# Float32 from the two words of a double: an integer add on Pool in place of two VectorE instructions

## The chip, the cores and the metric

The kernel runs on one core of a Trainium2 chip. Such a core has TensorE (matmuls), VectorE, ScalarE and Pool (GpSimd), which work side by side, each through its own instructions in order, and wait for each other by semaphores; SyncE issues the transfers. In the profile they are PE, DVE, ACT, POOL and SP. The metric is the time of one execution on the device in microseconds. The kernel before takes 1402.88 us, the median of three runs (1402.10 to 1403.73).

## The reference

Attention in chunks of 64 positions, then two feed-forward layers. The weights come as float64; the output is float32.

```python
scores = scale * np.matmul(q_c, k_c.transpose(0, 1, 2, 4, 3))   # 8 x 8 heads, 9 chunks of 64, head_dim 64
scores = scores - np.max(scores, axis=-1, keepdims=True)
attn = np.exp(scores)
attn = attn / (np.sum(attn, axis=-1, keepdims=True) + 1e-09)
out = np.matmul(attn, v_c)
x = out.transpose(0, 2, 1, 3).reshape(4608, 512)
h = np.maximum(np.maximum(x @ w1, x @ w2), x @ w3)               # 512 x 768 each
y = h @ w_out                                                    # 768 x 512
h = np.maximum(y @ w_in, 0.0)                                    # 512 x 2048
out = h * h @ w_out2                                             # 2048 x 512
```

## The kernel before, in words

The 4608 tokens are nine blocks of 512. A float32 operand is kept as two parts, hi (rounded to TensorE's fp32r) and lo (the rest), and a product of two operands is three matmuls: hi·hi, hi·lo, lo·hi. All weights are cut into tiles of 128 x 512: 24 for phase 1 (for each of six slices f of d_ff, three of w1, w2, w3 and one of w_out), 32 for phase 2 (w_in and w_out2).

**A weight tile** comes from HBM as `raw`, 128 x 512 pairs of 32-bit words: w0 is the low word of the double, w1 the high word. `convert` (L91 to L123) makes float32 of them. It is a generator; each `yield` ends a step, and the code that drives it decides what stands between two steps. In order: ScalarE takes the absolute value of the high word (Abs, L103); VectorE clamps it (L105), shifts it by 3 bits (L107) and puts the sign and the top exponent bit back (L110), which gives `a`, the value cut off below the high word's bits; ScalarE copies `a` to hi (L112); VectorE takes a's sign and exponent (L114) and multiplies the low word, as a number, by them (L116), which gives `s`; Pool subtracts hi from `a` (L122) and adds `s` (L123), which gives lo. For a tile of phase 2 (`hi is None`) Pool adds `s` to `a` in two halves (L120).

**The first phase** (everything up to about 185 us) is in the order in which it is written; a scheduler orders what comes later. For each of the first eight attention tiles there is a loop (L619 to L648): xl of the tile before (L341, VectorE), the transpose T of the softmax numerators e (L307, TensorE), a maximum (L285) and its subtraction (L288) two tiles ahead, three steps of a weight tile, a chunk of the products p, the products X (L330), scores S three tiles ahead, the sum of the next tile's e (L295) and its reciprocal rs (L298, L300), Pool's e*rs (L301), which the next T needs, the last steps of the weight tile, and Abs of the next one. ScalarE copies T to SBUF (et, L311) and X to xh (L336).

**Behind the loops** `flow` takes the other 16 tiles of phase 1 through their steps, three or four steps for each chunk of 24 matmuls: in a tile's third step, after L110 and hi, it also issues Abs of the next tile. Between the steps stand the ends of the products: for w1 ScalarE's copy s (L383), for w2 the maximum m (L386), for w3 the maximum h (L390), its hi part hh (L392, ScalarE) and hl (L394). Products p have two PSUM banks, so a chunk waits until the end of the one before the last has been read. y (L355 too) are the products with w_out.

Then come phase 2's operands (parked in HBM and fetched back), and its products z (L449) and o (L500). Temporary tiles of `convert`, s, m and h rotate through eight buffers.

Of the kernel before, what the change touches and what calls it, by code (L numbers as in the profile page):

```python
# [9 lines left out]
F32 = mybir.dt.float32  # L10
F32R = mybir.dt.float32r
BF16 = mybir.dt.bfloat16
U32 = mybir.dt.uint32
AF = mybir.ActivationFunctionType
ALU = mybir.AluOpType
# [26 lines left out]
def kernel(ctx: ExitStack, tc, qkv, w123, w_out, w_in2, w_out2, out):  # L42


    nc = tc.nc
# [10 lines left out]
    def tmp(name):  # L56
        return ap.tile([P, 512], F32, tag="t", name=name, bufs=NTMP)
# [24 lines left out]
    def halved(t):  # L82
        return t.rearrange("p (a c) -> p a c", a=2)
# [6 lines left out]

    def convert(raw, hi, lo):  # L91

        w0, w1 = raw[:, :, 0], raw[:, :, 1]
        a = tmp("a")
        s = tmp("s")  # L100
        au, su = a.bitcast(U32), s.bitcast(U32)
        v = nc.vector
        nc.scalar.activation(a, w1.bitcast(F32), AF.Abs)  # L103
        yield
        v.tensor_scalar(out=a, in0=a, scalar1=E_INF, scalar2=E_ZERO, op0=ALU.min, op1=ALU.max)  # L105
        yield
        v.tensor_scalar(out=au, in0=au, scalar1=3, scalar2=0x3FFFFFFF,  # L107
                        op0=ALU.logical_shift_left, op1=ALU.bitwise_and)
        yield
        v.scalar_tensor_tensor(out=au, in0=w1, scalar=0xC0000000, in1=au, op0=ALU.bitwise_and, op1=ALU.bitwise_or)  # L110
        if hi is not None:
            nc.scalar.copy(hi, halved(a))  # L112
        yield
        v.tensor_scalar(out=su, in0=au, scalar1=0xFF800000, scalar2=None, op0=ALU.bitwise_and)  # L114
        yield
        v.scalar_tensor_tensor(out=s, in0=w0, scalar=2.0**-52, in1=s, op0=ALU.mult, op1=ALU.mult)  # L116
        if hi is None:
            for h, part in enumerate(lo):
                c = slice(h * HC, h * HC + HC)
                nc.gpsimd.tensor_tensor(out=part, in0=a[:, c], in1=s[:, c], op=ALU.add)  # L120
            return
        nc.gpsimd.tensor_tensor(out=halved(a), in0=halved(a), in1=hi.bitcast(F32), op=ALU.subtract)  # L122
        nc.gpsimd.tensor_tensor(out=lo, in0=halved(a), in1=halved(s), op=ALU.add)  # L123

    def unit_steps(src, name, keep, late=False):


        if late:
            hi, lo = [shifted(name + n).rearrange("p (a c) -> p a c", a=2)[:, :, SH:] for n in "hl"]
        else:  # L130
            hi, lo = [halved(wp.tile([P, 512], F32R, tag="w", name=name + n)) for n in "hl"]
        keep(hi, lo)
        if src.dtype == F32:
            raw = ap.tile([P, 512], F32, tag="in", name="raw", bufs=4)
            nc.sync.dma_start(raw, src)
            yield
            split(halved(raw), hi, lo)
        else:
            raw = ap.tile([P, 512, 2], U32, tag="in", name="raw", bufs=4)
            nc.sync.dma_start(raw.rearrange("p n w -> p (n w)"), src.bitcast(U32))  # L140
            yield
            yield from convert(raw, hi, lo)
# [38 lines left out]
    def park(n, g):  # L181

        src = (lambda f: w_in2[f]) if n == "wi" else (lambda f: w_out2[f * P:(f + 1) * P, :])
        d = parked[n, g] = dp.tile([7, 2, P, 512], F32, name=f"{n}{g}d")
        q = [halved((level if n == "wi" and i < N0 else operand)(f"q{i}").bitcast(F32)) for i in range(4)]

        for r in range(2):
            for a in range(2):
                s, parts = src(2 * g + a + 8 * r), [x[:, a, :] for x in q[2 * r:2 * r + 2]]
                if s.dtype == F32:  # L190
                    for h in range(2):
                        nc.sync.dma_start(parts[h], s[:, h * HC:h * HC + HC])
                    yield
                else:
                    raw = ap.tile([P, 512, 2], U32, tag="in", name="raw", bufs=4)
                    nc.sync.dma_start(raw.rearrange("p n w -> p (n w)"), s.bitcast(U32))
                    yield
                    for k, _ in enumerate(convert(raw, None, parts)):
                        if k in (0, 2):
                            yield  # L200
                    yield
        for i, x in combine(q, n == "wi", nc.gpsimd):
            yield
            hi, lo = operand("ph"), operand("pl")
            nc.scalar.copy(halved(hi), x)
            yield
            nc.vector.tensor_tensor(out=halved(lo), in0=x, in1=halved(hi).bitcast(F32), op=ALU.subtract)  # L207
            nc.sync.dma_start(d[i - 1, 0], hi.bitcast(F32))
            nc.sync.dma_start(d[i - 1, 1], lo.bitcast(F32))
# [245 lines left out]
    def take(tag, name):  # L455
        t = tmp(name)
        nc.scalar.copy(t, bank[tag])  # L457
        return t
# [279 lines left out]
    for b in range(NB):  # L738
        for g in range(NG):
            bank["at"] = None  # L740
            z(b, g, 1, "at", True)
            a, s1 = bank["at"], take("at", "s1")
# [97 lines left out]
```

## Time and profile before

| | |
|---|---|
| median of 3 runs | 1402.88 us (1402.10 to 1403.73) |
| span of the profiled execution | 1401.4 us |
| TensorE busy | 1376.2 us (98%) |
| VectorE busy | 963.6 us (69%) |
| ScalarE busy | 492.4 us (35%) |
| Pool busy | 237.4 us (17%) |

The span runs from the first to the last instruction. Busy shares are means over stages with different limits: VectorE's 69% is 95% in one stage and far less in others. A wait is read from a row's end, "[3.26 <-ACT s L383]": the engine sat idle for 3.26 us before this instruction, until ScalarE's instruction of line 383, which wrote s, was done.

### The profile page before, as it was taken

What the parts mean: (1) busy time and instruction counts of PE and PEld (TensorE: products, weight loads), DVE (VectorE), ACT (ScalarE), POOL (GpSimd) and SP (SyncE); (2) the same over time, 40 slices, a digit from 0 to 9 for tenths busy, and PEclk for the clock granted to TensorE, in tenths of its full rate; (3) what the DMA queues carried; (4) which work ended last, traced back from release to release, by engine and by line L of the source; (5) the groups of instructions that cost most, each with busy time, mean ns of one, the idle gap of its engine ahead of it and who ended that gap; (6) DMA issues with size and microseconds to landing.
All of it is one profiled execution on the core that took longest, in us unless ns stands there. A gap on an engine that the chain in (4) does not pass through costs nothing.

```text
span 1401.4 us, 32734 instructions
## 1 busy us (share of the span) xinstructions
PE 1376.2 (98%) x13719; PEld 1358.6 (97%) x13719; DVE 963.6 (69%) x1525; ACT 492.4 (35%) x848; POOL 237.4 (17%) x204
## 2 busy tenths in 40 slices
PE   8889999999999999999999999999999999999998
PEld 5889999999999999999999999999999999999998
DVE  7998657677758577723266666666677888877774
ACT  3433233332323332411133333333334444444442
POOL 3654213332514323300000000000000000000000
PEclk9999999999999999999999999999999999999999
DMA  9332244653735554626643343343498444334341
GB/s 281 100 103 91 95 133 136 219 174 106 263 129 174 196 189 137 248 70 212 195 146 134 136 149 139 136 149 138 178 350 307 144 143 137 128 129 150 123 140 41
DMA packets 101236, 222.33 MB, mean 159 GB/s; under 512 B 11232, under 2 KB 20448, under 8 KB 101088
## 3 DMA queue, kind: packets, MB, share of 16 engines
q1 hardware_dynamic: 101088, 220.25, 46.1%
q8 instruction: 107, 1.75, 0.5%
q14 instruction: 41, 0.34, 0.1%
HBM read 134.22 MB, written 85.98 MB: 157 GB/s over the span
## 4 chain that ended last, share of the span: by engine, by line
PE 85%; DVE 1%; issue 0%; POOLq 0%; POOL 0%; ACT 0%; DVEq 0%; ACTq 0%
PE o L500 25%; PE z L449 25%; PE p L355 24%; PE y L355 9%; PE X L330 1%; PE S L278 1%; PE T L307 1%; DVE pl L207 0%; DVE u L472 0%; POOL u L472 0%; POOLq L836 0%; DVE mx L285 0%; DVE sm L295 0%; DVE e L288 0%; DVE h L390 0%
## 5 line engine op out<-in xcount | busy, mean ns | idle before, releaser
L449 PE MATMUL z<-yxh,wih 128*128 128x256 f32 x560 | 154.9, 277 | 0.0
L449 PE MATMUL z<-yxh,wil 128*128 128x256 f32 x560 | 154.7, 276 | 0.0
L449 PE MATMUL z<-yxl,wih 128*128 128x256 f32 x560 | 154.7, 276 | 0.0
L500 PE MATMUL o<-wo2h,gl 128*128 128x256 f32 x504 | 140.7, 279 | 0.0
L472 POOL TENSOR_TENSOR u<-u,s 128x512 f32<-128x512 f32 x9 | 11.7, 1296 | 761.5 <-DVE u L472 761.5
L500 PE MATMUL o<-wo2h,gh 128*128 128x256 f32 x504 | 140.4, 279 | 0.0
L500 PE MATMUL o<-wo2l,gh 128*128 128x256 f32 x504 | 140.2, 278 | 0.0
L500 PE MATMUL o<-wo2h,gxl 128*128 128x256 f32 x504 | 140.1, 278 | 0.0
L500 PE MATMUL o<-wo2h,gxh 128*128 128x256 f32 x504 | 139.9, 278 | 0.0
L500 PE MATMUL o<-wo2l,gxh 128*128 128x256 f32 x504 | 139.9, 278 | 0.0
L472 DVE TENSOR_TENSOR c<-z,s 128x512 f32<-128x512 f32 x108 | 74.3, 688 | 89.2 <-PE z L449 84.7
L449 PE MATMUL z<-yh,wih 128*128 128x256 f32 x448 | 124.2, 277 | 0.0
L449 PE MATMUL z<-yh,wil 128*128 128x256 f32 x448 | 124.1, 277 | 0.0
L449 PE MATMUL z<-yl,wih 128*128 128x256 f32 x448 | 124.1, 277 | 0.0
L392 ACT CAST hh<-h 128x512 fp32r<-128x512 f32 x54 | 33.5, 621 | 220.4 <-DVE h L390 209.4
L390 DVE TENSOR_TENSOR h<-p,m 128x512 f32<-128x512 f32 x54 | 37.1, 687 | 107.0 <-PE p L355 107.0
L457 ACT COPY s<-z 128x512 f32<-128x512 f32 x108 | 63.3, 586 | 133.7 <-PE z L449 132.4
L449 PEld LDWEIGHTS z<-yxh,wih 128*128 128x128 f32 x560 | 105.2, 188 | 0.2 <-DVE c L472 0.2
L449 PEld LDWEIGHTS z<-yxh,wil 128*128 128x128 f32 x560 | 105.1, 188 | 0.0
L449 PEld LDWEIGHTS z<-yxl,wih 128*128 128x128 f32 x560 | 105.1, 188 | 0.0
L500 PEld LDWEIGHTS o<-wo2l,gh 128*128 128x128 f32 x504 | 94.9, 188 | 0.0
L500 PEld LDWEIGHTS o<-wo2h,gl 128*128 128x128 f32 x504 | 94.7, 188 | 0.0
(196 smaller groups left out, 4160.1 us busy)
## 6 DMA issues: line engine op xcount, KB each, us to landing
gd<-g SPq DMA_DIRECT2D x144, 256.0 KB, 2.0
gr<-gd SPq DMA_DIRECT2D x72, 512.0 KB, 4.2
qk<-in_qkv SPq DMA_DIRECT2D x28, 512.0 KB, 4.3
raw<-in_w_out SPq DMA_DIRECT2D x22, 512.0 KB, 5.0
raw<-in_w SPq DMA_DIRECT2D x18, 512.0 KB, 3.5
v<-in_qkv SPq DMA_DIRECT2D x72, 128.0 KB, 5.9
yd<-ys SPq DMA_DIRECT2D x36, 256.0 KB, 2.8
yr<-yd SPq DMA_DIRECT2D x18, 512.0 KB, 5.0
```

Source lines behind the costliest of these rows:

```text
L278: nc.tensor.matmul(s_t[t][o:o + D, h ^ t % 2, :], lhsT=q[r, h, :], rhs=k[r, h, :], start=True, stop=True,)
L307: nc.tensor.transpose(tp[:, p * P:(p + 1) * P], e[:, 2 * p:2 * p + 2, :].rearrange("p h k -> p (h k)"), ident)
L330: nc.tensor.matmul(xps_t[t][j * D:j * D + D, p, c * D:c * D + D], lhsT=v[o:o + D, c, p, :], rhs=et[o:o + D, p, q:q + D], start=True, stop= ...
L355: nc.tensor.matmul(dst[:, c], lhsT=lhs, rhs=rhs[:, c], start=first and i == 0 and j == 0, stop=last and j == len(pairs) - 1, skip_group_ch ...
L390: nc.vector.tensor_tensor(out=h, in0=p, in1=st[b], op=ALU.max)
L392: nc.scalar.copy(hh, h)
L449: nc.tensor.matmul(dst[:, a * HC:a * HC + HC], lhsT=l[:, a, w], rhs=r[:, k, :], start=first and a + k + j == 0, stop=j == 2, skip_group_ch ...
L457: nc.scalar.copy(t, bank[tag])
L472: (eng or nc.vector).tensor_tensor(out=t, in0=x, in1=y, op=ALU.add)
L500: nc.tensor.matmul(bank[i][:, m * HC:m * HC + HC], lhsT=l[:, a, t], rhs=r[:, a, :], start=g + m + a + j == 0, stop=g == NG - 1 and j == 2, ...
```

## The change

`convert` no longer makes `s`. ScalarE copies the low word, as a number, times 2 to the power -29, to an integer tile `r` (this is the rounded carry into the low bits of the float32); Pool adds `r` to the bits of `a` as integers; only then does ScalarE copy hi, and Pool subtracts hi from the sum. VectorE's L114 and L116 go. A tile's conversion has one step less, so its last step is empty where the loops and `flow` still take it.

```diff
         w0, w1 = raw[:, :, 0], raw[:, :, 1]
         a = tmp("a")
-        s = tmp("s")
-        au, su = a.bitcast(U32), s.bitcast(U32)
+        r = tmp("r")
+        au, ru = a.bitcast(U32), r.bitcast(U32)
         v = nc.vector
         nc.scalar.activation(a, w1.bitcast(F32), AF.Abs)
+        nc.scalar.activation(ru, w0, AF.Copy, scale=2.0**-29)
         yield
...
         v.scalar_tensor_tensor(out=au, in0=w1, scalar=0xC0000000, in1=au, op0=ALU.bitwise_and, op1=ALU.bitwise_or)
-        if hi is not None:
-            nc.scalar.copy(hi, halved(a))
-        yield
-        v.tensor_scalar(out=su, in0=au, scalar1=0xFF800000, scalar2=None, op0=ALU.bitwise_and)
-        yield
-        v.scalar_tensor_tensor(out=s, in0=w0, scalar=2.0**-52, in1=s, op0=ALU.mult, op1=ALU.mult)
         if hi is None:
             for h, part in enumerate(lo):
                 c = slice(h * HC, h * HC + HC)
-                nc.gpsimd.tensor_tensor(out=part, in0=a[:, c], in1=s[:, c], op=ALU.add)
+                nc.gpsimd.tensor_tensor(out=part.bitcast(U32), in0=au[:, c], in1=ru[:, c], op=ALU.add)
             return
-        nc.gpsimd.tensor_tensor(out=halved(a), in0=halved(a), in1=hi.bitcast(F32), op=ALU.subtract)
-        nc.gpsimd.tensor_tensor(out=lo, in0=halved(a), in1=halved(s), op=ALU.add)
+        nc.gpsimd.tensor_tensor(out=au, in0=au, in1=ru, op=ALU.add)
+        nc.scalar.copy(hi, halved(a))
+        yield
+        nc.gpsimd.tensor_tensor(out=lo, in0=halved(a), in1=hi.bitcast(F32), op=ALU.subtract)
```

What this moves on Pool, in the attention loops. Before (e and rs belong to the softmax; w0_0, w1_0, w2_0 are the first three weight tiles):

```order
L301 TENSOR_TENSOR e_198<-e_198,rs_211 128x512
L301 TENSOR_TENSOR e_208<-e_208,rs_301 128x512
L122 TENSOR_TENSOR a_201<-a_201,w0_0h_119 128x512
L123 TENSOR_TENSOR w0_0l_120<-a_201,s_202 128x512
L301 TENSOR_TENSOR e_258<-e_258,rs_384 128x512
L122 TENSOR_TENSOR a_308<-a_308,w1_0h_133 128x512
L123 TENSOR_TENSOR w1_0l_134<-a_308,s_309 128x2x256
```

The same place in the changed kernel, where line 112 is the integer add, 115 the subtraction and 293 the product e*rs:

```order
L293 TENSOR_TENSOR e_198<-e_198,rs_212 128x512
L112 TENSOR_TENSOR a_201<-a_201,r_202 128x512
L115 TENSOR_TENSOR w0_0l_120<-a_201,w0_0h_119 128x512
L293 TENSOR_TENSOR e_209<-e_209,rs_303 128x512
L112 TENSOR_TENSOR a_307<-a_307,r_308 128x512
L115 TENSOR_TENSOR w1_0l_134<-a_307,w1_0h_133 128x2x256
L293 TENSOR_TENSOR e_260<-e_260,rs_385 128x512
```

A loop's e*rs stood ahead of the tile's two instructions and now stands behind them.

On ScalarE, behind the loops, before (L112 is hi, L103 the next tile's Abs, L383 the copy s, L392 hh):

```order
L112 CAST w0_2h_752<-a_935 128x512
L103 ACTIVATE a_1003<-raw_859 128x512
L383 COPY s1_1040<-p0_861 128x512
L112 CAST w1_2h_857<-a_1003 128x2x256
L103 ACTIVATE a_1045<-raw_940 128x512
L112 CAST w2_2h_938<-a_1045 128x512
L103 ACTIVATE a_1112<-raw_1037 128x512
L392 CAST hh_1118<-h_1116 128x512
```

And in the changed kernel (L113 is hi, L98 Abs, L99 the new copy, L375 s, L384 hh):

```order
L113 CAST w0_2h_747<-a_927 128x512
L98 ACTIVATE a_997<-raw_853 128x512
L99 ACTIVATE r_998<-raw_853 128x512
L375 COPY s1_1032<-p0_855 128x512
L113 CAST w1_2h_851<-a_997 128x2x256
L98 ACTIVATE a_1038<-raw_933 128x512
L99 ACTIVATE r_1039<-raw_933 128x512
L113 CAST w2_2h_931<-a_1038 128x512
L98 ACTIVATE a_1104<-raw_1029 128x512
L99 ACTIVATE r_1105<-raw_1029 128x512
L384 CAST hh_1111<-h_1109 128x512
```

Their sequence is kept and one copy comes in for each tile; hi, at the head of it, now follows Pool's add and no longer VectorE's L110.

## Rows read from the trace of the kernel before

**Rows 1.** The page, busy us, share of the span and instructions of each engine

```profile
PE 1376.2 (98%) x13719; PEld 1358.6 (97%) x13719; DVE 963.6 (69%) x1525; ACT 492.4 (35%) x848; POOL 237.4 (17%) x204
```

**Rows 2.** Windows: length, busy time of each engine, granted clock, DMA share, GB/s

```profile
60.00:120.00 60.00, 51.18 (x428) 49.91 (x427) 56.93 (x73) 20.34 (x36) 32.47 (x22) 0.94 0.32 102
120.00:155.00 35.00, 34.35 (x352) 33.95 (x351) 26.99 (x39) 9.63 (x16) 16.63 (x12) 1.00 0.27 84
155.00:700.00 545.00, 543.95 (x6190) 538.09 (x6189) 326.19 (x542) 160.95 (x284) 134.76 (x124) 1.00 0.51 169
```

**Rows 3.** Waits, 0 to 155 us: who waited for whom, total, times, longest

```profile
PE T L307 <- POOL e L301: 6.8, 5, 2.6
```

**Rows 4.** Timeline of TensorE: start, us, instruction, idle time before it

```profile
30.49 0.77 PE L307 MATMUL T<-ident,e 128*128 128x128 f32 x4 [2.55 <-POOL e L301]
...
57.19 0.66 PE L307 MATMUL T<-ident,e 128*128 128x128 f32 x4 [0.52 <-POOL e L301]
...
84.54 0.51 PE L355 MATMUL p<-xh,w_1h 128*128 128x256 f32 x2 [3.26 <-ACT s L383]
...
116.34 0.79 PE L355 MATMUL p<-xh,w_3h 128*128 128x256 f32 x2 [2.29 <-ACT s L383]
```

**Rows 5.** Timeline of VectorE, one attention loop

```profile
26.97 0.69 DVE L110 SCALAR_TENSOR_TENSOR a<-raw,a 128x512 uint32<-128x512 uint32 x1
...
28.78 0.20 DVE L300 RECIPROCAL rs<-sm 128x8 f32<-128x8 f32 x1
...
30.65 1.30 DVE L105 TENSOR_SCALAR a<-a 128x512 f32<-128x512 f32 x1
...
33.42 0.69 DVE L110 SCALAR_TENSOR_TENSOR a<-raw,a 128x512 uint32<-128x512 uint32 x1
```

**Rows 6.** Timeline of Pool, the same loop

```profile
29.06 1.38 POOL L301 TENSOR_TENSOR e<-e,rs 128x512 f32<-128x512 f32 x1 [2.41 <-DVE rs L300]
30.40 1.27 POOL L122 TENSOR_TENSOR a<-a,w_0h 128x512 f32<-128x512 f32 x1
31.75 1.34 POOL L123 TENSOR_TENSOR w_0l<-a,s 128x512 fp32r<-128x512 f32 x1
```

**Rows 7.** Timeline of all engines, one tile behind the loops

```profile
65.71 0.41 DVE L105 TENSOR_SCALAR a<-a 128x512 f32<-128x512 f32 x1
...
66.61 0.69 DVE L110 SCALAR_TENSOR_TENSOR a<-raw,a 128x512 uint32<-128x512 uint32 x1
...
67.34 0.62 ACT L112 CAST w_2h<-a 128x512 fp32r<-128x512 f32 x1 [3.95 <-DVE a L110]
67.41 0.43 DVE L114 TENSOR_SCALAR s<-a 128x512 uint32<-128x512 uint32 x1
...
67.87 0.71 ACT L103 ACTIVATE a<-raw 128x512 f32<-128x512 f32 x1
...
68.04 1.68 POOL L122 TENSOR_TENSOR a<-a,w_2h 128x512 f32<-128x512 f32 x1 [3.40 <-ACT w_2h L112]
...
68.61 1.40 DVE L105 TENSOR_SCALAR a<-a 128x512 f32<-128x512 f32 x1
...
71.47 0.69 DVE L110 SCALAR_TENSOR_TENSOR a<-raw,a 128x512 uint32<-128x512 uint32 x1
```

**Rows 8.** Groups by line, 0 to 560 us: busy us, mean ns

```profile
L116 DVE SCALAR_TENSOR_TENSOR s<-raw,s 128x512 f32<-128x512 uint32 x56 | 45.9, 830 | 0.5
...
L103 ACT ACTIVATE a<-raw 128x512 f32<-128x512 f32 x56 | 37.3, 673 | 43.2 <-DMA raw<-in_w_in 21.3 <-DMA raw<-in_w_out 13.2 <-issue 7.8
...
L114 DVE TENSOR_SCALAR s<-a 128x512 uint32<-128x512 uint32 x56 | 25.0, 466 | 1.0
```

**Rows 9.** Timeline of VectorE and ScalarE: a copy s, a later L110

```profile
82.10 0.69 DVE L110 SCALAR_TENSOR_TENSOR a<-raw,a 128x512 uint32<-128x512 uint32 x1
...
83.92 0.57 ACT L383 COPY s<-p 128x512 f32<-128x512 f32 x1
...
118.65 0.69 DVE L110 SCALAR_TENSOR_TENSOR a<-raw,a 128x512 uint32<-128x512 uint32 x1
```

## The prediction, made before the changed kernel had run

> **What bounds the kernel now.** I read the busy table first: TensorE is busy for 1376.2 of 1401.4 us [rows 1], so everything there is to win or lose lies in some 25 us of its idle time and in any new idle time. The windows say where [rows 2]: from 155 us on TensorE is busy for 543.95 of 545 us; from 60 to 120 us it is busy for only 51.18 of 60, and VectorE there for 56.93, with a granted clock of 0.94. The first 155 us are the stretch that decides. Two of its waits matter: the transposes T wait for Pool's product e*rs, 6.8 us in five waits [rows 3], and the products p wait for ScalarE's copy s. Single waits are in [rows 4]: T at 30.49 waited 2.55 us; p at 84.54 and at 116.34 waited 3.26 and 2.29 us for s, and behind the second one a pair of matmuls takes 0.79 us, against 0.51 behind the first, which is the lower clock level (1.2 GHz). So in this stretch TensorE follows VectorE, which converts the 24 weight tiles of phase 1, one after another, between the attention steps and the maxima.
>
> **What the change does to a tile.** VectorE loses the mask L114 and the product L116: 25.0 + 45.9 us over 56 tiles [rows 8], start to start some 0.9 us a tile in the attention loops, and 1.1 us (67.41 is L114's start, 68.61 the next tile's L105) later on. ScalarE gains one copy of a tile with a stride, as L103, which takes 673 ns [rows 8], about 0.53 us start to start. Pool keeps two instructions a tile, but the add comes first, then ScalarE's copy hi, then the subtraction. Three consequences, all of order and not of load:
> 1. hi now waits for Pool's add, and on ScalarE the next tile's Abs stands right behind hi. Before, hi needed only L110.
> 2. In the loops Pool's e*rs stands behind the add and the subtraction of the tile, where it stood ahead of both.
> 3. xh and s, on ScalarE behind hi, wait as well.
>
> The new add is in no row. The nearest are Pool's float32 instructions of two full inputs: 1.27 to 1.35 us alone, 1.68 when a VectorE instruction interferes [rows 6, 7]. Far ends: 0.69, VectorE's own two-input L110, and 2.7, twice the 1.34 of a Pool row, if integers are added in two passes. I take 1.3, the row it is nearest to. The Trainium skill (GPSIMD Engine Reference, Performance versus the Vector engine) puts a two-input Pool loop at about 2.6 cycles an element because both reads share a port, and that floor does not depend on the arithmetic; an estimate from it is 512 x 2.6 / 1.2 GHz = 1.11 us, and with it the sum below would come out some 4 us lower. No run here shows an integer add.
>
> **The attention loops (11 to 65 us).** Count from the start of L110 in one loop. Before: e*rs starts at 29.06 - 26.97 = 2.1 us, T at 30.49 - 26.97 = 3.5 us, and the next L110 comes at 33.42, 6.45 later [rows 4, 5, 6]. After: the add starts when L110 (0.69) is done and 0.2 has passed, at 0.9, and ends at 2.2; hi takes 2.25 to 2.87; the subtraction 2.95 to 4.25; e*rs 4.3 to 5.65; T starts at 5.7. T is thus 2.2 us later against L110. On VectorE the loop goes: xh on ScalarE behind hi, 2.78 to 3.37; xl at 3.42; the maximum at 4.02; L105 at 4.62. There e*rs is running, and L105 is held by a running Pool instruction: it takes 1.30 at 30.65 and 1.40 at 68.61, in each case to 0.3 past Pool's end, but 0.41 with Pool idle [rows 5, 6, 7]. So L105 ends at 5.95; the subtraction of the maximum at 5.87, L107 at 6.47, next L110 at 6.93. The loop grows from 6.45 to 6.93, although VectorE has 0.9 us less to do: it now waits for xh. Seven loops give 7 x 0.48 = 3.4 us (my walk, loop by loop, gives 3.2, as the first loops lose less and the fifth more, where the maximum m waits for products behind the late T). The eighth T then stands at 57.19 + 3.2 + 2.2, some 5.5 us later, and TensorE's idle time ahead of the T grows to 1.4 to 2.6 us each, so the clock may drop more than once. The first product that needs all of X, and the L110 of the next tile (66.61 before [rows 7]), come at about +5.1: VectorE has caught up a little.
>
> **The sixteen tiles behind the loops (66 to 150 us).** Before, one tile takes 71.47 - 66.61 = 4.86 us where nothing else stands between, all of it VectorE's [rows 7]; hi starts at +0.73, the next Abs at +1.26 and ends at +1.97, while VectorE is still in L116: Abs is never late. After, from L110's start: add 0.9 to 2.2, hi at 2.25, Abs at 2.78 to 3.45, L105 at 3.5. Pool's subtraction, begun at 2.95 when hi is done, is then running, stretched to 1.68 as at 68.04, so L105 ends at 4.9; L107 takes 0.46 start to start, and L110 comes at 5.4. The ring L110, add, hi, Abs, L105, L107, L110 passes through three engines and takes 5.4 us a tile in place of 4.86. Maxima and subtractions of phase 1 that stand behind L110 use VectorE's idle time and cost nothing; those between L105 and L110, and an hl that waits for an hh behind the late hi, lengthen a tile to 6.0 to 6.9. For the ten tiles from 66.61 to 118.65 [rows 7, 9] I get five at 5.4 and five at 6.0 to 6.9, 59.1 us against 52.05: +7. Last, a copy s behind hi, Abs and the new copy leaves at 3.8 after L110; at 83.92 it left 1.8 after the L110 at 82.10 [rows 9]: +2.0 for the product that waits for its buffer, as the one at 116.34 does. So at that point TensorE is 5.1 + 7 + 2 = 14 us late, with waits of 5 us or so at the places of the 3.26 and 2.29.
>
> **Behind it.** From 120 us TensorE is busy 34.35 of 35 and then all the time [rows 2]; nothing there gives the delay back. The 32 tiles of phase 2's weights gain and lose the same instructions under products that keep TensorE busy; its whole idle time from 155 to 700 us is 1.05 us, so at most that can be won, and without that cover a tile would cost the ring's 0.5 us. I cost them at nothing.
>
> **The sum.** 1401.4 + 14 = 1415.4 us for the span. The profiled span stands 1.5 us under the median of the runs, 1402.88, which has what lies around it; so I forecast 1417 us. With the add at 1.27 and hand-overs at 0.08 (28.78 + 0.20 to Pool's 29.06) in place of 0.2, 22 tiles give 3 us back; with the add at 1.68 they take 8 more: its own range is 1411 to 1426.
>
> **Rivals.**
> - *VectorE's relief pays.* For it: VectorE is 95% busy from 60 to 120 us, and TensorE's waits trail it. If nothing replaces it, some 18 tiles up to 120 us give back 0.9 each, 16 us, at most: 1387; half of it, 1395, is likelier, as TensorE then bounds. Against it: the next Abs stands behind hi, which waits for Pool, in the order of ScalarE's instructions. Chance 0.10.
> - *The port is not in the way.* If L105 starts between Pool's two instructions, at 0.41, the tile's ring is 4.4, under the 4.86 of before; ten tiles win 4.6 us and the loop is 6.0, so that the later T and the s cost about what is won: 1401 to 1406. Against it: every L105 in [rows 5, 7] that met Pool at work was held. Chance 0.08.
> - *The integer add is slow*, at 2.7 us. Then each of the 22 tiles takes 1.4 longer, 31 us: about 1448. For it: no integer instruction of Pool stands in the trace. Chance 0.08.
> - The forecast has 0.74. That the change does not do what it says can't be: in its order of instructions no L114 or L116 is left, and the new copy stands there for all 56 tiles.
>
> **How the numbers follow.** The first rival is faster by more than 0.2%, 2.8 us, about what can be told from no change; the second is split, mostly within it; the other two are slower. That makes 0.10, 0.07 and 0.83. The range, 1404 to 1428, holds the forecast with its unknown add and part of the second rival, and leaves out the first and the third.
>
> **What would show it.** Right: VectorE's busy time falls by some 70 us in all and its share from 60 to 120 us to about three quarters, with L105 waiting for ScalarE's Abs; hi waits for Pool; T waits for e*rs by 2 us and more in each loop; TensorE's idle time is near 38 us, all of the gain of it ahead of 155 us; L110 to L110 is 5.4 us or more. Wrong: VectorE's tiles follow each other in under 4.8 us, or L105 takes 0.4 beside Pool (second rival), or the add's row is far from 1.3.

## The result, and the profile after

The changed kernel takes 1413.07 us, the median of four runs (1411.27 to 1414.47), against 1402.83 us for the kernel before beside it (1402.10 to 1403.73): a ratio of 1.0064, with a 95% interval of 1.0049 to 1.0078. It is slower by 10 us. The forecast was 1417 us, the range 1404 to 1428.

The page of the kernel after (busy us, share of the span, instructions), to be held against [rows 1]; its span is 1410.0 us:

```profile
PE 1375.9 (98%) x13719; PEld 1358.2 (96%) x13719; DVE 892.6 (63%) x1413; ACT 521.0 (37%) x904; POOL 223.3 (16%) x204
```

VectorE has lost 71.0 us of work and TensorE has the same 13719 matmuls in about the same busy time, but the span is 8.6 us longer: TensorE's idle time went from 25.2 to 34.1 us. The windows of the kernel after (length, busy time of each engine, granted clock, DMA share, GB/s), beside [rows 2], say where:

```profile
60.00:120.00 60.00, 50.17 (x432) 48.76 (x432) 29.92 (x47) 23.29 (x41) 27.32 (x21) 0.94 0.30 91
120.00:155.00 35.00, 30.60 (x236) 30.40 (x237) 15.20 (x26) 13.59 (x24) 14.33 (x12) 0.90 0.28 89
155.00:700.00 545.00, 543.74 (x6244) 537.88 (x6243) 299.15 (x477) 177.55 (x314) 131.23 (x126) 1.00 0.50 166
```

From 60 to 120 us VectorE is now busy for 29.92 of 60 us, where it was for 56.93; it no longer sets the pace, and TensorE is no faster. Behind 155 us hardly anything differs. What TensorE waits for, 0 to 160 us (total, times, longest), beside [rows 3]:

```profile
PE p L347 <- ACT s L375: 12.8, 5, 5.9
PE T L299 <- POOL e L293: 10.4, 6, 2.7
```

The timeline of TensorE in the kernel after, beside [rows 4] (start, us, instruction, idle time before it):

```profile
31.86 0.66 PE L299 MATMUL T<-ident,e 128*128 128x128 f32 x4 [2.48 <-POOL e L293]
...
59.96 0.66 PE L299 MATMUL T<-ident,e 128*128 128x128 f32 x4 [1.21 <-POOL e L293]
...
89.05 0.80 PE L347 MATMUL p<-xh,w_1h 128*128 128x256 f32 x2 [5.88 <-ACT s L375]
...
122.49 0.72 PE L347 MATMUL p<-xh,w_3h 128*128 128x256 f32 x2 [2.90 <-ACT s L375]
...
148.32 0.51 PE L347 MATMUL p<-xh,w_4h 128*128 128x256 f32 x2 [1.91 <-ACT s L375]
```

The same points one under the other show how the delay grows:

| point | before | after | later by |
|---|---|---|---|
| eighth T | 57.19 | 59.96 | 2.8 |
| L110 (after: L106) of the first tile behind the loops | 66.61 | 68.84 | 2.2 |
| p that waits for s | 84.54 | 89.05 | 4.5 |
| L110 (L106) ten tiles on | 118.65 | 122.97 | 4.3 |
| p that waits for s | 116.34 | 122.49 | 6.2 |
| p that waits for s | 140.84 | 148.32 | 7.5 |
| next T of the attention | 185.35 | 194.24 | 8.9 |

The loop after, VectorE's timeline beside [rows 5]:

```profile
26.70 0.69 DVE L106 SCALAR_TENSOR_TENSOR a<-raw,a 128x512 uint32<-128x512 uint32 x1
27.32 0.68 DVE L287 TENSOR_REDUCE sm<-e 128x8 f32<-128x512 f32 x1
...
29.98 0.69 DVE L333 TENSOR_TENSOR xl<-X,xh 128x512 fp32r<-128x512 f32 x1 [0.83 <-ACT xh L328]
...
31.18 0.91 DVE L101 TENSOR_SCALAR a<-a 128x512 f32<-128x512 f32 x1
...
33.06 0.69 DVE L106 SCALAR_TENSOR_TENSOR a<-raw,a 128x512 uint32<-128x512 uint32 x1
```

and Pool's, beside [rows 6]:

```profile
27.54 1.27 POOL L112 TENSOR_TENSOR a<-a,r 128x512 uint32<-128x512 uint32 x1 [2.09 <-DVE a L106]
29.54 1.27 POOL L115 TENSOR_TENSOR w_0l<-a,w_0h 128x512 fp32r<-128x512 f32 x1 [0.73 <-ACT w_0h L113]
30.76 1.05 POOL L293 TENSOR_TENSOR e<-e,rs 128x512 f32<-128x512 f32 x1
```

The order is the one forecast: add, hi, subtraction, and only then e*rs. The loop takes 33.06 - 26.70 = 6.36 us (before 6.45), and T starts 31.86 - 26.70 = 5.16 us after L106 (before 3.5). A tile behind the loops, all engines, beside [rows 7]:

```profile
68.84 0.69 DVE L106 SCALAR_TENSOR_TENSOR a<-raw,a 128x512 uint32<-128x512 uint32 x1
...
69.68 1.30 POOL L112 TENSOR_TENSOR a<-a,r 128x512 uint32<-128x512 uint32 x1 [5.32 <-PE p L347]
...
71.01 0.62 ACT L113 CAST w_2h<-a 128x512 fp32r<-128x512 f32 x1 [4.33 <-POOL a L112]
...
71.53 0.66 ACT L98 ACTIVATE a<-raw 128x512 f32<-128x512 f32 x1
...
71.71 1.29 POOL L115 TENSOR_TENSOR w_2l<-a,w_2h 128x512 fp32r<-128x512 f32 x1 [0.73 <-ACT w_2h L113]
...
72.30 0.97 DVE L101 TENSOR_SCALAR a<-a 128x512 f32<-128x512 f32 x1 [2.77 <-ACT a L98]
...
73.31 0.43 DVE L103 TENSOR_SCALAR a<-a 128x512 uint32<-128x512 uint32 x1
...
73.77 0.69 DVE L106 SCALAR_TENSOR_TENSOR a<-raw,a 128x512 uint32<-128x512 uint32 x1
```

This is the ring: L106, Pool's add, hi, Abs, L101, L103, L106. VectorE sits idle for 2.77 us in it, waiting for Abs, which stands behind hi, which waits for Pool. It takes 4.93 us, where VectorE's own five instructions took 4.86. The groups of Pool's add and of L101, 0 to 160 us, with what ended the idle time before them, say the same of the stretch: the add takes 1300 ns in the mean of 24 tiles, and all of L101's idle time, 22.8 us in ten waits behind the loops, ends with Abs (the 24 waits in the expectation of e1 below are the number of tiles):

```profile
L112 POOL TENSOR_TENSOR a<-a,r 128x512 uint32<-128x512 uint32 x24 | 31.2, 1300 | 59.2 <-DVE a L106 51.8 <-PE p L347 5.3 <-ACT hh L384 2.1
...
L101 DVE TENSOR_SCALAR a<-a 128x512 f32<-128x512 f32 x24 | 17.4, 726 | 22.8 <-ACT a L98 22.8
```

### The profile page after: what moved, and what is told of

It reads as the page before. It is cut to its first block, busy times and chain, and to the rows that moved or that the text cites. A ratio compares the mean times of both kernels' runs of the same rounds, so it can differ in the third digit from the quotient of the medians.

```text
span 1410.0 us, 32701 instructions
## 1 busy us (share of the span) xinstructions
PE 1375.9 (98%) x13719; PEld 1358.2 (96%) x13719; DVE 892.6 (63%) x1413; ACT 521.0 (37%) x904; POOL 223.3 (16%) x204
## 4 chain that ended last, share of the span: by engine, by line
PE 85%; DVE 1%; issue 0%; POOLq 0%; POOL 0%; ACT 0%; DVEq 0%; ACTq 0%
PE o L492 25%; PE z L441 24%; PE p L347 24%; PE y L347 9%; PE X L322 1%; PE S L270 1%; PE T L299 1%; DVE pl L199 0%; DVE u L464 0%; POOL u L464 0%; POOLq L828 0%; DVE mx L277 0%; DVE sm L287 0%; DVE e L280 0%; DVE h L382 0%
## 5 line engine op out<-in xcount | busy, mean ns | idle before, releaser
L464 POOL TENSOR_TENSOR u<-u,s 128x512 f32<-128x512 f32 x9 | 11.7, 1296 | 761.6 <-DVE u L464 761.6
L384 ACT CAST hh<-h 128x512 fp32r<-128x512 f32 x54 | 33.5, 621 | 241.3 <-DVE h L382 224.2
```

What stands on the lines that cost most here:

```text
L384: nc.scalar.copy(hh, h)
L464: (eng or nc.vector).tensor_tensor(out=t, in0=x, in1=y, op=ALU.add)
```

## The experiments

Theory: the loss is order, not load. (a) hi, behind Pool's add, holds up ScalarE's queue and with it the next Abs; (b) e*rs behind two Pool instructions makes T late. Rivals: ScalarE's added copy; and for the size that I got wrong, chance or another cause of Pool's 1.68 us. All ratios are to the kernel before, timed on the same chip.

**Abs ahead of hi, behind the loops (e1_abs_first).** The change, with the next tile's Abs and copy issued one step earlier:

```diff
                 go(u)
-                if i == 2:
+                if i == 1:
                     go(*ahead[:1])
```

> The changed kernel, but behind the loops the next tile's Abs and the new copy are issued one step earlier, so on ScalarE they stand ahead of the tile's hi. Theory (the ring L110, add, hi, Abs, L105): it opens; VectorE's L105 no longer waits for Abs (22.8 us in 24 waits in the changed kernel), a tile takes 3 to 4 us in place of 4.93, TensorE's waits for s (12.8 us) shrink to 4 or less, and the time falls by 8 to 14 us, to 1399 to 1405 us. Rival (the new copy is too much for ScalarE): its work is the same, so 1412 to 1414 us as the changed kernel. The attention loops are unchanged: the eighth T stays near 60 us.

Measured: 1400.93 us (1399.81 to 1402.25), 0.9986 [0.9976, 0.9995]. One line about the order of ScalarE takes back 12 us, all of the loss and a little more, with the added copies still there. VectorE's timeline, from the first tile behind the loops to the tenth after it:

```profile
70.80 0.69 DVE L106 SCALAR_TENSOR_TENSOR a<-raw,a 128x512 uint32<-128x512 uint32 x1
...
73.30 0.69 DVE L106 SCALAR_TENSOR_TENSOR a<-raw,a 128x512 uint32<-128x512 uint32 x1
...
116.65 0.69 DVE L106 SCALAR_TENSOR_TENSOR a<-raw,a 128x512 uint32<-128x512 uint32 x1
```

Ten tiles take 45.9 us in place of 54.1, and L101 waits for Abs for 2.0 us in two waits behind the loops, in place of 22.8 in ten. TensorE's waits for s fall to 5.7 us in three, not to the 4 or less that I expected. In the loops this run has the change's own sequence of instructions; even so the first L106 behind them stands at 70.80 and not at 68.84 (behind the T at 39.15 the granted clock fell, see the last section). Points in the loops thus move by 2 us between two executions, and a difference of that size between two traces shows little by itself.

**e*rs ahead of the subtraction, in the loops (e2_product_first).**

```diff
-        go(n, u, n, n, u)
+        go(n, n, n, u, u)
```

> The changed kernel, but in the attention loops Pool's e*rs is issued ahead of the tile's subtraction (hi still behind the add). Theory: T follows 3.6 us behind L110 and no longer 5.2, the eighth T comes at 58 to 59 us in place of 59.96, but xh still stands behind hi, and what T wins is partly lost to the ring behind the loops: 1410.5 to 1412.5 us. Rival (the order on Pool makes the whole loss): back to 1403 to 1405 us.

Measured: 1406.79 us (1406.48 to 1409.45), 1.0030 [1.0017, 1.0043]: 6.3 us less than the change, more than the theory gave and less than the rival. The first L106 behind the loops is back at 66.60, as before the change (66.61); the tiles behind it still take 4.92. The profiled execution is the slowest of the five (1409.45 us): its next T, at 191.87, is only 2.4 us ahead of the change's, so the trace shows a part of what the median wins.

**Both, by giving hi a step of its own (e3_hi_own_step).** e2, and hi in the step behind Pool's add, so that xh and the next Abs stand ahead of it on ScalarE, in the loops too:

```diff
         nc.gpsimd.tensor_tensor(out=au, in0=au, in1=ru, op=ALU.add)
-        nc.scalar.copy(hi, halved(a))
         yield
+        nc.scalar.copy(hi, halved(a))
```

> The changed kernel with both orders mended: hi becomes a step of its own behind Pool's add, so that on ScalarE xh and the next tile's Abs stand ahead of it, and in the loops e*rs stands ahead of the subtraction. The same instructions and sizes as in the changed kernel. Theory: VectorE's 0.9 us a tile now pays: TensorE's waits before 155 us fall from 30 us to some 10, 1388 to 1397 us, faster than both. Rival (an extra copy on ScalarE or Pool's add as such costs the time): 1408 us or more.

Measured: 1390.3 us (1389.8 to 1391.4), 0.9913 [0.9898, 0.9927]: faster than both kernels, by 13 and 23 us. Its window from 60 to 120 us:

```profile
60.00:120.00 60.00, 57.00 (x491) 56.41 (x488) 40.47 (x55) 31.29 (x54) 33.61 (x25) 1.00 0.37 113
```

TensorE is busy for 57.00 of 60 us at a granted clock of 1.00, where it had 51.18 and 0.94 before. Its idle time ahead of 155 us is 11.7 us, against 28.2 in the changed kernel and 18.8 before. So VectorE's relief was worth something; the order ate it, and 10 us on top.

**The own step alone (e7_own_step_only).** The second edit without the first.

> The changed kernel with one edit: hi becomes a step of its own behind Pool's add, so that on ScalarE xh and the next tile's Abs are issued ahead of it; e*rs stays behind the tile's Pool instructions. If the ring through hi and Abs and the late e*rs add up independently, the 16.5 us from 1406.8 to 1390.3 are found here too: 1395 to 1399 us. Rival: once hi is out of the way, Pool's order is the only thing left that holds T, and the gain is smaller, 1400 to 1405; or larger (Pool has slack in the loops then, e*rs costs nothing): 1389 to 1392.

Measured: 1401.18 us (1398.88 to 1405.58), 0.9987 [0.9976, 0.9998]. The four corners are 1413.1 (neither), 1406.8 (e*rs), 1401.2 (hi) and 1390.3 (both): -6.3 and -11.9 alone, -22.8 together, so 4.6 more than their sum. The two do not add up independently; the time lies in the rival's smaller gain, 1400 to 1405. Its first L106 behind the loops stands at 76.19, against 65.02 with both. Windows in one loop of this run (columns as above) show what is special:

```profile
32.00:34.00 2.00, 1.13 (x6) 1.13 (x6) 1.97 (x4) 0.00 (x0) 0.85 (x2) 0.50 1.12 272
34.00:36.00 2.00, 2.00 (x11) 2.00 (x11) 1.45 (x3) 1.11 (x2) 1.25 (x1) 0.50 0.99 271
36.00:38.00 2.00, 2.00 (x35) 1.78 (x38) 0.00 (x0) 0.00 (x0) 0.00 (x0) 0.50 0.54 215
```

Behind a wait of 2.98 us for the T at 32.87 the granted clock is 0.50, the lower of the two levels (1.2 GHz), for some 6 us. TensorE is then fully busy, and ScalarE and VectorE wait for X: xh starts at 38.49 and the next L106 at 42.45, 9.32 us behind the one at 33.13, where the loop before took 6.85. It happens a second time behind the T at 42.18. Two such loops would account for 5 us, about the 4.6 that the two edits give beyond their sum; that was not tested by itself, and it rests on one execution of ten.

**e*rs ahead of the add too (e9_product_before_add).** e3, with one step of the weight tile less ahead of X, which puts rs and e*rs ahead of L106's add:

```diff
-            go(m, u, m, u, u)
+            go(m, u, m, u)
```

> The run with hi as a step of its own and e*rs ahead of the subtraction (1390.3 us), with rs and e*rs in the loops moved ahead of L106 and the integer add as well, so that Pool makes e*rs first of its three instructions, as in the kernel before. Theory: the T waits go from 4.3 us in five to under 2, and as TensorE's idle time there is on the path: 1386 to 1390. Rival: the weight tile's L106 comes 0.7 to 1 us later in each loop, the first L106 behind the loops too, and VectorE's delay outweighs the earlier T: 1391 to 1396.

Measured: 1398.04 us (1396.77 to 1401.55), 0.9968 [0.9957, 0.9979]: 7.7 us worse than e3, the rival's side and beyond it. The timeline of one loop of this run, Pool and ScalarE:

```profile
37.76 1.38 POOL L293 TENSOR_TENSOR e<-e,rs 128x512 f32<-128x512 f32 x1 [2.40 <-DVE rs L292]
...
39.10 1.28 POOL L112 TENSOR_TENSOR a<-a,r 128x512 uint32<-128x512 uint32 x1
...
40.41 0.62 ACT L114 CAST w_1h<-a 128x512 fp32r<-128x512 f32 x1 [2.99 <-POOL a L112]
...
42.05 0.57 ACT L303 COPY et<-T 128x512 f32<-128x512 f32 x1
```

T waits less (3.9 us in three waits), but the add now stands behind e*rs, hi behind the add, and et behind hi, Abs and r: T is done at 39.84, and its copy starts 2.2 us later. TensorE waits 4.3 us for et instead, and a loop takes 7.02 us (L106 at 37.60 and 44.62). Whichever instruction waits for Pool at the head of ScalarE's queue, what is behind it pays.

**The order of Pool alone, with the old arithmetic (e6_product_last).** The kernel before, with e*rs behind the tile's two Pool instructions:

```diff
-        go(n, u, n, n, u)
+        go(n, u, n, u, n)
```

> The kernel before with its old arithmetic, and only the order of Pool in the eight attention loops changed: e*rs is issued behind the tile's subtraction and addition and no longer ahead of them. Theory (the late e*rs alone costs a good part of what the change loses): the T wait 2 us or so more each, the eighth T stands 3 to 5 us later than 57.19, part of it is caught up behind the loops as VectorE sets the pace there: 1405 to 1409 us. Rival (the place of e*rs matters only together with the late hi): the T waits grow, but VectorE stays the bound, the first L110 behind the loops stands within 1 us of 66.61, and the time is 1402 to 1404.

Measured: 1409.56 us (1404.46 to 1411.31), 1.0046 [1.0030, 1.0061]: a loss, half a us above the theory's 1405 to 1409. Its trace has T waits of 11.7 us in seven (6.8 in five before), and the first L110 behind the loops at 68.82, which is the changed kernel's 68.84. The profiled execution is the one of 1404.46 us, so its trace shows less of the loss than the median has: p at 118.84 is 2.5 us late, the one at 141.78 only 0.9. The medians show that the order alone costs 6 us, and the T waits that it does so in the loops. That the loops' 2.2 us come to just the changed kernel's may be chance, as such points move by 2 us between executions; what the other executions lose behind the loops is not shown.

**ScalarE's copy alone (e4_copy_alone).** The kernel before with a copy like r for each tile, to a tile that nothing reads:

```diff
         nc.scalar.activation(a, w1.bitcast(F32), AF.Abs)
+        nc.scalar.activation(junk, w0, AF.Copy, scale=2.0**-29)
```

> The kernel before with the new ScalarE copy added for all 56 tiles, its result unused (written as bytes, to a tile of its own). Everything else as before. Theory (load on ScalarE does not matter, order does): 1402 to 1405 us, within 0.2% of before. Rival (the copy's 0.66 us a tile on ScalarE is what makes the changed kernel slow): 1409 us or more.

Measured: 1406.65 us (1404.68 to 1408.89), 1.0026 [1.0017, 1.0035]: between theory and rival. Some 3.4 us can be ScalarE's load; I had put this at nothing by itself ("all of order and not of load"). The trace shows little of where they arise: TensorE waits for s 7.5 us in three, 6.2 before, but the profiled execution is the fastest of the ten (1404.68). e1 and e3 carry the same copies and are faster than the kernel before; what the copy costs in the changed kernel itself is not shown.

**A two-input VectorE instruction put back (e5_two_input_back).** The change, with an instruction in the form of the removed L116 behind L106; nothing reads its result:

```diff
         v.scalar_tensor_tensor(out=au, in0=w1, scalar=0xC0000000, in1=au, op0=ALU.bitwise_and, op1=ALU.bitwise_or)
+        v.scalar_tensor_tensor(out=junk, in0=w0, scalar=2.0**-52, in1=w1, op0=ALU.mult, op1=ALU.mult)
```

> The changed kernel, with one VectorE instruction of two full inputs (the form of the removed product: the two words of the double, 128 x 512, result written to a byte tile that nothing reads) put right behind L106. Theory: in the kernel before, Pool's instructions took 1.6 to 1.7 us where such a two-input VectorE instruction was in flight as they started, and the change took that away, which is why I sized the tile too long. With it back, the integer add, which starts some 0.85 us after L106, goes from 1.30 to about 1.65 us, a tile behind the loops from 4.93 to about 5.3, and the time to 1416 to 1420 us, near what I predicted for the change. Rival: the 1.68 had another reason (the held L105 itself, or chance): the add stays at 1.27 to 1.31, the tile at 4.9 to 5.0 and the time at 1412 to 1414.

Measured: 1419.83 us (1418.89 to 1420.20), 1.0117 [1.0098, 1.0135]. Timeline of VectorE and Pool in one tile behind the loops (L108 is the change's L106, L109 the added instruction, L115 the add, L118 the subtraction, L103 the clamp that waits for Abs):

```profile
72.00 0.69 DVE L108 SCALAR_TENSOR_TENSOR a<-raw,a 128x512 uint32<-128x512 uint32 x1
...
72.61 0.68 DVE L109 SCALAR_TENSOR_TENSOR junk<-raw 128x512 uint8<-128x512 uint32 x1
...
72.83 1.60 POOL L115 TENSOR_TENSOR a<-a,r 128x512 uint32<-128x512 uint32 x1 [5.01 <-PE p L350]
...
75.16 1.27 POOL L118 TENSOR_TENSOR w_2l<-a,w_2h 128x512 fp32r<-128x512 f32 x1 [0.73 <-ACT w_2h L116]
...
75.75 0.97 DVE L103 TENSOR_SCALAR a<-a 128x512 f32<-128x512 f32 x1 [2.46 <-ACT a L100]
...
77.21 0.69 DVE L108 SCALAR_TENSOR_TENSOR a<-raw,a 128x512 uint32<-128x512 uint32 x1
```

and the group of the add, 0 to 160 us:

```profile
L115 POOL TENSOR_TENSOR a<-a,r 128x512 uint32<-128x512 uint32 x23 | 36.7, 1596 | 59.1 <-DVE a L108 52.0 <-PE p L350 5.0 <-ACT hh L387 2.1
```

The add goes from 1300 to 1596 ns, the mean of 23 tiles, the subtraction, which meets no such instruction, stays at 1.27, and the ring from 4.93 to 5.21. Behind the loops VectorE's extra 0.6 us is itself no cost: its clamp still waits 2.46 us for Abs at 75.75. So the durations are shown. The time is a weaker sign: 3.2 of the 6.8 us by which this run is slower than the change stand already at the first tile behind the loops (72.00 against 68.84), and what of them is VectorE's added load there was not told apart.

## Why the prediction was right, and where it was not

**Direction and mechanism: right.** The loss is the ring through hi and Abs behind the loops and e*rs behind two Pool instructions in them. Undoing the one (e1) or the other (e2) takes back 12 and 6 us; both are in the rows: L101 waits for Abs, hi for Pool, T for e*rs by 2.4 to 2.7 us in three loops running (2 us and more in each were forecast; the other three waits are 0.65 to 1.21). VectorE's busy time fell by 71 us, where 70 were forecast, but its share from 60 to 120 us fell to half and not to three quarters. Of the 27 us that it lost there 14.4 are L114 and L116; most of the rest is the clamp, the shift and hl, which a running Pool instruction lengthened less often (the shift's mean went from 1073 to 489 ns). A part of the 95% before was VectorE being held and not work, which I had not taken apart. The rival that VectorE's relief pays fell for this order; with the order mended (e3) it is what happens, at 1390, between its 1387 and 1395. The rival in which the port is not in the way fell: L101 takes 0.91 and 0.97 us beside Pool, not 0.41. The rival of a slow integer add fell: 1.30 us, as I took it. The Trainium skill's floor for two-input loops (GPSIMD Engine Reference, Performance versus the Vector engine) holds in that the arithmetic does not matter, 1.30 for integers and 1.29 for the float32 subtraction; my estimate of 1.11 us from it was low.

**The size: the failed term is Pool's durations.** I took 1.68 for the subtraction "as at 68.04" and 1.35 for e*rs (1.38 in [rows 6]), from rows of the kernel before. In that kernel those instructions started while VectorE's L116 was in flight; the change removes L116. Timeline of VectorE beside e*rs at 29.06 [rows 6] and the subtraction at 68.04 [rows 7], then of Pool and VectorE in a later tile:

```profile
28.90 0.64 DVE L116 SCALAR_TENSOR_TENSOR s<-raw,s 128x512 f32<-128x512 uint32 x1
...
67.87 0.69 DVE L116 SCALAR_TENSOR_TENSOR s<-raw,s 128x512 f32<-128x512 uint32 x1
...
77.73 1.30 POOL L122 TENSOR_TENSOR a<-a,w_2h 128x512 f32<-128x512 f32 x1 [1.74 <-ACT w_2h L112]
...
78.04 1.53 DVE L116 SCALAR_TENSOR_TENSOR s<-raw,s 128x512 f32<-128x512 uint32 x1
```

Where L116 is first, Pool takes 1.68; where Pool is first, it takes 1.30 and L116 is held from 0.69 to 1.53. The prediction says that 1.68 is Pool's time "when a VectorE instruction interferes"; it did not ask which one, nor whether the change takes it away, and it takes e*rs at 1.35, near a row that L116 lengthened as well. e5 shows it: with such an instruction back the add takes 1.60 and the ring 5.21. The Trainium skill says so (SBUF — State Buffer, Who interferes with whom): a VectorE instruction with two SBUF inputs and a GpSimd instruction that reads SBUF exclude each other, and the one that starts first keeps the port to its end. The rows agree in both directions; by that page the subtraction had to be taken at 1.30 and the ring at 5.0.

Term by term:
- The tile behind the loops: 5.4 forecast, 4.93 measured. Subtraction started at 2.87 after L106 (2.95 forecast) and ended at 4.16 (4.63), L101 at 4.43 (4.9): 0.39 of the 0.47 is the stretch that was not there, the rest shorter hand-overs. L101 was held to 0.27 past Pool's end, as forecast. Ten tiles: 54.1 in place of 59.1, +2.1 us and not +7.
- The loop: 6.93 forecast, 6.36 measured, shorter than before and not longer. e*rs takes 1.05 and not 1.35, and starts 0.24 earlier, so L101, which is held by it, is done 0.6 us earlier. T is later against L106 by 1.6 us (2.2 forecast), the eighth T by 2.8 (5.5), the first L106 behind the loops by 2.2 (5.1); these two are points of single executions, which move by 2 us.
- s: 3.8 after L106 forecast, 88.44 - 84.67 = 3.77 measured. Right; and the p that follows waits 5.88 us, as the "5 us or so" said; the second such place, at 122.49, waits 2.90.
- The sum up to there: 14 us forecast, 6.2 measured (p at 122.49).
- Behind it: nothing forecast, 2.7 us measured (8.9 at the next T). The ring goes on to the last tiles: p at 148.32 waits 1.91 us, where the one at 140.84 waited 0.65, and the granted clock from 120 to 155 us is 0.90, where it was 1.00. I had read the end of the stretch from the busy share of before, which could not show a wait that comes later.
- Phase 2's tiles cost nothing, as forecast: 543.74 us busy of 545.
- ScalarE's added copy: forecast at nothing by itself; e4 puts up to 3.4 us on it, in the order of before.
- The sum's own range, 1411 to 1426, does not follow from its two terms, which give 1414 to 1425.

So the 4 us between 1417 and 1413 are what is left of misses of opposite sign: 8 us too much up to 122 us, most of it from Pool's durations (an estimate: 3.9 us in ten tiles, some 2 in seven loops), 2.4 too little behind it, and 1.6 too little from the profiled span to the median, which stands 3.1 us above it and not 1.5. That the total comes so near is in part luck.

## What to carry to other kernels

Ask of every instruction moved to another engine which in-order queue its consumer heads: here the consumer's place on ScalarE, one line, was worth 12 us, and a step of its own, with one product issued earlier on Pool, turned a loss of 10 us into a gain of 13. Work taken off the engine that sets the pace pays only when no chain through the others takes its place. A duration read from a trace belongs to its neighbours: when the change removes the neighbour, take the row without it.

## What the runs showed of the hardware that was not expected

- A Pool instruction that starts while a two-input VectorE instruction is in flight is lengthened, in these rows by some 0.7 of what is left of it: 1.27 to 1.60 us with 0.46 left of L109 at 72.83 (e5), 1.30 to 1.68 with 0.52 left at 68.04 and 1.04 to 1.38 with 0.48 left at 29.06 (before). Two inputs are not needed: in e3 the subtraction starts together with the one-input clamp L101 and takes 1.55, where it takes 1.27 to 1.29 with Pool alone. A VectorE reduction does not do this: in the kernel after, the add at 27.54 started with L287 in flight (27.32 to 28.00) and took 1.27. The rows of e3:

```profile
30.27 0.41 DVE L101 TENSOR_SCALAR a<-a 128x512 f32<-128x512 f32 x1
30.27 1.55 POOL L115 TENSOR_TENSOR w_0l<-a,w_0h 128x512 fp32r<-128x512 f32 x1
```

- The integer add of Pool on 128 x 512 words takes as long as its float32 instructions: 1.30 us. ScalarE's copy of strided 32-bit words to integers takes what Abs takes: 659 ns, mean of 24, beside 666.
- TensorE's waits of 2 to 3 us are not all worth the same, and their length does not tell which are dear. Behind those of 2.98 and 2.78 us in e7 the granted clock was 0.50 and some 0.6 for a loop's products, and the first such loop took 9.32 us in place of 6.85. It fell behind a wait of 2.46 us in e1, too, and stayed at 1.00 behind one of 3.01 in e5 and behind those of 2.4 to 2.7 us in the kernel after. The T and a window (columns as above) of e1:

```profile
39.15 1.12 PE L299 MATMUL T<-ident,e 128*128 128x128 f32 x4 [2.46 <-POOL e L293]
...
40.00:42.00 2.00, 2.00 (x12) 2.00 (x11) 1.93 (x4) 1.11 (x2) 0.82 (x1) 0.50 0.00 0
```

and of e5:

```profile
27.05 0.66 PE L302 MATMUL T<-ident,e 128*128 128x128 f32 x4 [3.01 <-POOL e L296]
...
26.00:44.00 18.00, 11.39 (x236) 10.73 (x238) 15.91 (x28) 8.05 (x15) 10.28 (x8) 1.00 0.74 206
```
